# Odd chunks normalised before the second marker, and their loads moved in an mLSTM + FFN kernel

## The chip, the cores and the metric

The kernel runs on one core of a Trainium2 chip. Its time is device time in microseconds (us) for one launch. Engines are called as in the profile: PE is TensorE (PEld its weight loads), DVE is VectorE, ACT is ScalarE, POOL is GpSimd, SP is SyncE, which here only issues DMAs. Each engine works its own list of instructions strictly in order; an instruction that waits for a semaphore holds all that stand behind it on that engine.

## The reference

Two blocks are computed one after the other. The first is an mLSTM cell over 4 batches, 8 heads, 768 tokens and a head dimension of 40; the second is a feed-forward block with a squared ReLU, 3072 tokens by 320, with 2048 hidden units.

```python
# per batch and head, for every token t:
m_new = maximum(f_gate + m, i_gate)
f_stab = exp(f_gate + m - m_new);  i_stab = exp(i_gate - m_new)
C = f_stab * C + i_stab * outer(v, k)
n = f_stab * n + i_stab * k
y = sigmoid(o_gate) * (C @ q) / maximum(abs(n . q), 1)
# then, with x = y as (3072, 320):
h = maximum(x @ w_in, 0)
out = (h * h) @ w_out
```

Inputs and outputs are float32.

## The kernel before

The 3072 tokens are cut into 24 chunks of 128 tokens (six chunks per batch, all 8 heads of a chunk together). Within a chunk the recurrence is written as attention: scores k·q, weighted by exponentials of gate sums, plus the contribution of the state C that the chunk before left. The feed-forward block works on 12 groups of two chunks.

The main loop (L1440) goes through `parts`, four quarters (`at` 0 to 3) to a phase, one phase to a chunk s = 6, 7, 8, and so on. In even phases PE computes FFN2 of a group (seven products with sums of operands, `ffn2_fast`, L1066), in odd phases FFN1 of a later group (`ffn1_open` and `ffn1_close`, L1145 and L1178, twice each, also with sums of operands). The attention of the same chunk is woven in. The order on every engine is the order in which this loop writes the instructions down; no scheduler changes it. From chunk 10 on, even chunks are `joined` (L1437): the first half of their attention is done at the end of the odd phase before.

In the odd phase of chunk s (9 to 21) with `joined(s + 1)`, group g of FFN1:

- quarter 0: `ffn1_open(g, 0)`.
- quarter 1: attention of chunk s (`attend_begin`, first marker; `attend_end`), then on SP `store_num`, `load_A`, `load_num`: the numerators N of chunk s go to DRAM and come back turned. `ffn1_close(g, 0)`.
- quarter 2: weights of chunk s + 1, `ffn1_open(g, 1)`, the turn of the squares of k and q (`turn_kq`, L406), then S2 (`sums(g - 1, ..., (2,))`, L1056): S2 = S1 - A11, an operand of the second product of the next FFN2. POOL issues the loads of k and v of the even chunk s + 3.
- quarter 3: on SP `load_squares(s + 3)` (L399); `ffn1_close(g, 1)` with `attend_begin(s + 1)` in its middle. At the end of `attend_begin` stands a marker (L792): DVE reads the last number that PE has written and writes a spare word of k, which the next matmuls of the second half read; so this half starts behind the marker. Behind it DVE makes the four closing sums (L1192 to L1195). Then comes `normalise_turned(s)` (L890 to L903, nine DVE instructions: x = N, gated and divided), `store_rows(s)` (L931) and `load_o(s + 5)` (L414).

In the even phase of chunk s + 1 that follows:

- quarter 0: `attend_end(s + 1)`, then `mask` and `decay_C` of chunk s + 2 on POOL (L479, L768), the loads of k and v of the odd chunk s + 4 on POOL (L363 to L375, seven issues), and on SP `store_num(s + 1)`, `load_A(s + 3)`, `load_rows(s)` (L936, four issues: x of the odd chunk comes back from DRAM in squares), `load_num(s + 1)` (L878).
- quarter 2: `turn_squares(s)` on DVE (L943) finishes the turning of x; `normalise_turned(s + 1)`.
- quarter 3: `sums_of_x` on POOL (L1132, L1135) makes, from x of two chunks, the operands `xs` in `lent_t`, which the second block of matmuls of the next FFN1 reads (L1140).

Of the kernel before, what the change touches and what calls it, by code (L numbers as in the profile page):

```python
# [29 lines left out]
def kernel(  # L30
# [30 lines left out]
    NB = S // P  # L61
# [7 lines left out]
    NPAIR = NF // 2  # L69
# [853 lines left out]
    def xT_half(s):  # L923
        g, j = divmod(s, GT)
        if j == 0:
            st["xT", g] = xts.tile([P, GT, 3, P], F32, name="xT")
        return st["xT", g][:, j]

    def store_rows(s):
        t = st[s]["xT"] = xT_half(s).rearrange("p c t -> p (c t)")  # L930
        nc.sync.dma_start(x_d[s].rearrange("c t d -> t c d"), st[s]["x"][:].rearrange("p (c d) -> p c d", c=3))  # L931

    def load_rows(s):
        t = st[s]["xT"]
        for r in range(P // SQ):
            nc.sync.dma_start(  # L936
                t[r * SQ : (r + 1) * SQ].rearrange("p (b a) -> p b a", a=SQ),
                x_d[s, :, :, r * SQ : (r + 1) * SQ].rearrange("c (n p) a -> p (c n) a", p=SQ),
            )

    def turn_squares(s):
        t = st[s]["xT"]
        nc.vector.transpose(t, t)  # L943
        del st[s]
# [268 lines left out]
    def do(f, s):  # L1213
        if 0 <= s < NT:
            f(s)
# [97 lines left out]
    for u in range(8):  # L1313
        s = 2 + u // 2
# [122 lines left out]
    def joined(s):  # L1437
        return EARLY <= s < NT and s % 2 == 0

    for n, (which, g, i) in enumerate(parts):  # L1440
        s, at = NB + n // 4, n % 4
        if n == len(ROUNDED):
            brought.close()
            late = ctx.enter_context(tc.tile_pool(name="late", bufs=1, side="right"))
        even = s % 2 == 0
        fast = which == 1
        if n == 2:
            half_tanh(6)
            half_tanh(7)
        if at == 3 and not even and s + 3 > EARLY:  # L1450
            do(load_squares, s + 3)
        if at == 0 and even and s < EARLY:
            do(scores, s)
            if n > 0:
                do(turn_kq, s + 1)
            do(weighted, s)
        if n == 0:
            turn_kq(7)
            pair_up(8)
            load_rows(4)  # L1460
            rounding.words()
            rounding.join()
        if at == (0 if joined(s) else 1):
            if not joined(s):
                do(attend_begin, s)
            if n == 5:
                sums_of_weights(3)
            if even:
                do(lambda s: scores(s, ("h" if s < EARLY else False, "h")), s + 1)
            if fast:  # L1470
                ffn1_rows(g, 0, True)
                if joined(s + 1):
                    scores(s + 1, (False, "h"))
            do(attend_end, s)
            do(decays, s + 1)
            if not even and s > EARLY + 1:
                do(half_tanh, s)
            do(mask, s + 1)
            if not even and not fast:
                do(turn_kq, s + 1)  # L1480
            do(decay_C, s + 1)
            if not fast and not even:
                do(turn_squares, s - 1)
            if even and s > NB:
                do(load, s + 3)
            do(store_num, s)
            if s > NB + 1:
                do(load_A, s + 2)
            if joined(s):
                load_rows(s - 1)  # L1490
            if n == 1:
                normalise_turned(5)
                store_rows(5)
                turn_squares(4)
            if n == 5:
                load_rows(6)
            do(load_num, s)
            if n == 1:
                load_rows(5)
                weigh(7, masked=True)  # L1500
                sums_of_win(2)
            if s + 2 <= EARLY:
                do(load_squares, s + 2)
            if even and s <= NB + 1:
                do(load_A, s + 2)
        if n == 3:
            load_o(8)
            load_o(9)
            sums_of_weights(0)
        if n == 8:  # L1510
            sums(1, slice(0, NPAIR), (3,))
        if n == 9:
            sums(1, slice(0, NPAIR), (4,))
            sums_of_weights(2)
            turn_squares(6)
        if which == 2 and i == 3 and g == NG - 2:
            sums(g + 1, slice(0, NPAIR), (2,))
        if which == 2 and g > 1 and i < 2:
            sums(g, slice(0, NPAIR), (3 + i,))
        if at == 3 and even and NB < s and s // 2 - 1 < NG:  # L1520
            sums_of_x(s // 2 - 1)
        if at == 2 and not fast:
            if even and n > 2 and not joined(s):
                do(turn_squares, s - 1)
            do(scale_q, s + 1)
        if at == (1 if joined(s) else 3) and joined(s + 2):
            turn_kq(s + 2)
        if at == 3:
            if s % 4 == 3 and s < EARLY:
                for r in range(s + 1, min(s + 5, NT) if n > 7 else 10):  # L1530
                    half_tanh(r)
        if n == 10:
            half_tanh(10)
            half_tanh(11)
        if fast:
            if i % 2:
                if n == 7:
                    sums(1, slice(0, NPAIR), (2,))
                early = (lambda: attend_begin(s + 1)) if at == 3 and joined(s + 1) else None
                ffn1_close(g, i // 2, i == 1, early)  # L1540
                if early:
                    normalise_turned(s)
                    store_rows(s)
                    do(load_o, s + 5)
                if at == 1:
                    if s + 1 < EARLY:
                        do(turn_kq, s + 1)
                    if n > 5:
                        do(turn_squares, s - 1)
            else:  # L1550
                if at == 2 and joined(s + 1):
                    weigh(s + 1, masked=True)
                    weighted(s + 1)
                ffn1_open(g, i // 2)
                if at == 2 and joined(s + 1):
                    do(scale_q, s + 1)
                    do(turn_kq, s + 2)
                if i == (2 if joined(s + 1) else 0) and g > 2:
                    sums(g - 1, slice(0, NPAIR), (2,))
            if at == 2 and not joined(s + 1):  # L1560
                do(scale_q, s + 1)
            if n == 6:
                sums(1, slice(0, NPAIR), (1,))
        elif g == 0:
            ffn2(i)
        else:
            ffn2_fast(g, i)
        if at == 2:
            if n > 2 and not joined(s + 1):
                do(lambda s: weigh(s, masked=True), s + 1)  # L1570
            if even and s > EARLY:
                do(half_tanh, s)
            if even and s + 3 > EARLY:
                do(lambda s: load_squares(s, nc.scalar), s + 3)
            ffn1_square()
            if even and joined(s):
                do(turn_squares, s - 1)
            if even:
                do(weighted, s + 1)
            if not joined(s + 1):  # L1580
                do(normalise_turned, s)
                do(store_rows, s)
            if n == 2:
                pair_up(9)
                turn_squares(5)
                sums_of_x(2)
                load(8)
            if not even and s <= NB + 1:
                do(load_A, s + 2)
            if n > 2 and not joined(s + 1):  # L1590
                do(load_o, s + 5)
                do(load_rows, s)
            if s == NB + 1:
                pair_up(s + 3)
        if n in (5, 6):
            load(4 + n)
            load_o(5 + n)
        if at == 2 and joined(s + 1):
            do(load, s + 3)
        if n in (4, 7):  # L1600
            pair_up(11 + n // 7)
        if at == 3 and (even and s >= EARLY or s == EARLY - 1):
            for r in (5, 6) if even else (4, 5):
                do(pair_up, s + r)
        if n == 4:
            sums_of_weights(1)
        if n == 3:
            turn_halves()
        if n in (7, 16):
            spread_slots(2 + n // 16)  # L1610
        if at == 0:
            ffn1_square()
        if n < len(ROUNDED):
            while rounding.done < ROUNDED[n]:
                rounding.step()
# [30 lines left out]
```

## Time and profile before

| | |
|---|---|
| median of 3 runs | 489.94 us (489.55 to 490.25) |
| the profiled execution, its own time | 486.3 us |
| its span in the profile | 484.6 us |
| PE busy, of the span | 472.9 us (98%) |
| PE weight loads | 441.7 us (91%) |
| DVE busy | 340.2 us (70%) |
| ACT, POOL busy | 243.4 us (50%), 222.3 us (46%) |
| granted PE clock | 1.0 |

The profile is of one execution. Times in it count from the start of the span. A row of a timeline has start and length in us, engine, line of the kernel, operation, output<-input with their sizes, how many instructions are merged, and in brackets how long the engine was idle before it and what ended that. A row of waits has who waited for whom, then total us, how often, and the longest. SPq, POOLq and ACTq are the DMA issues of an engine. Chunks and phases can be told apart by time: the odd phases of chunks 9 to 21 end at about 166, 202, 240, 277, 312, 350 and 386 us.

### The profile page before, as it was taken

Reading aid. Unit: us, or ns where it says so; the run is one execution under the profiler, and the core shown is the slowest. Engines: PE = TensorE matmul, PEld = TensorE weight load, DVE = VectorE, ACT = ScalarE, POOL = GpSimd, SP = SyncE. Lnnn points to the kernel's source line nnn. Section 1 sums busy time; section 2 is a strip of 40 time slices with the busy share of each in tenths; the row PEclk is TensorE's granted clock in tenths of the full one; section 3 lists DMA queues with packets and bytes.
Section 4 is the critical chain, followed back from the end, with each engine's and each line's share of the span. In section 5 each row is a group of like instructions: output and inputs, shape, how many; then the busy total and the mean of one; then the engine's idle time right before and its main releaser. Section 6 shows DMA issues by size and latency. Waiting matters only on the chain.

```text
span 484.6 us, 15673 instructions
## 1 busy us (share of the span) xinstructions
PE 472.9 (98%) x6387; PEld 441.7 (91%) x6389; DVE 340.2 (70%) x725; ACT 243.4 (50%) x534; POOL 222.3 (46%) x337
## 2 busy tenths in 40 slices
PE   8999999999998999998999999999999999999997
PEld 5876788779998999998999999999999999999997
DVE  7969768898885966855965965865965957635441
ACT  4598798635743543544553552553553551513300
POOL 5464544677881866556556546554553111020000
DMA  8999998789995697596897696896694223200000
GB/s 177 218 248 252 273 212 219 223 141 230 204 181 142 137 190 184 95 168 134 157 173 171 119 171 146 145 174 138 123 160 97 70 76 84 55 23 7 1 28 27
DMA packets 192839, 69.93 MB, mean 144 GB/s; under 512 B 158144, under 2 KB 181504, under 8 KB 192768
## 3 DMA queue, kind: packets, MB, share of 16 engines
q1 hardware_dynamic: 157424, 56.39, 54.4%
q0 software_dynamic: 6080, 10.16, 9.4%
q10 hardware_dynamic: 29264, 2.39, 4.8%
q8 instruction: 50, 0.82, 0.7%
q14 instruction: 21, 0.17, 0.1%
HBM read 55.69 MB, written 18.92 MB: 154 GB/s over the span
## 4 chain that ended last, share of the span: by engine, by line
PE 79%; DMA 9%; DVE 5%; ACT 3%; issue 1%; POOL 1%; SPq 1%; DVEq 0%; POOLq 0%
PE h_ps L1061 27%; PE h_ps L1140 23%; PE h_ps L1173 7%; PE h_ps L977 4%; PE h_ps L1015 4%; DMA kqT<-kq_rows 3%; PE numT L823 3%; PE numT L801 2%; DMA kq<-num_rows 2%; DMA og<-in_o_gate_dram 2%; PE tp L587 1%; PE numT L835 1%; DMA A_bc<-a_slots 1%; PE h_ps L988 1%; PE tp L595 1%
## 5 line engine op out<-in xcount | busy, mean ns | idle before, releaser
L1061 PE MATMUL h_ps<-T,S 128*128 128x160 f32 x352 | 51.4, 299 | 0.0
L1061 PE MATMUL h_ps<-w_out,g 128*128 128x160 f32 x336 | 48.9, 301 | 0.7 <-issue 0.7
L1061 PEld LDWEIGHTS h_ps<-T,S 128*128 128x128 f32 x352 | 49.0, 190 | 0.0
L1077 DVE TENSOR_TENSOR y_sb<-y_sb,h_ps 128x160 f32<-128x160 f32 x44 | 14.0, 319 | 48.5 <-PE h_ps L1061 48.5
L1061 PEld LDWEIGHTS h_ps<-w_out,g 128*128 128x128 f32 x336 | 46.2, 190 | 1.9 <-issue 1.5
L1154 ACT COPY r_sb<-h_ps 128x512 f32<-128x512 f32 x20 | 11.7, 584 | 66.0 <-DMA kqT<-kq_rows 31.4
L1140 PE MATMUL h_ps<-xT,w_in 128*128 128x128 f32 x320 | 43.3, 278 | 0.0
L1140 PE MATMUL h_ps<-lent_t,w_in 128*128 128x128 f32 x320 | 42.3, 275 | 0.0
L1173 PE MATMUL h_ps<-xT,w_in 64*64 64x128 f32 x960 | 39.5, 272 | 1.7 <-DVE r_sb L1156 1.7
L1140 PE MATMUL h_ps<-lent_t 128*128 128x128 f32 x320 | 39.2, 276 | 1.6 <-POOL lent_t L1135 1.6
L1140 PEld LDWEIGHTS h_ps<-xT,w_in 128*128 128x128 f32 x320 | 39.2, 192 | 1.6 <-issue 1.2
L1140 PEld LDWEIGHTS h_ps<-lent_t 128*128 128x128 f32 x320 | 37.3, 192 | 2.0 <-POOL lent_t L1135 2.0
L375 POOL DMA_DIRECT2D va<-in_v_dram x64 | 39.1, 621 | 0.0
L1140 PEld LDWEIGHTS h_ps<-lent_t,w_in 128*128 128x128 f32 x320 | 38.9, 192 | 0.0
L1132 POOL TENSOR_TENSOR lent_t<-xT 128x128 f32<-128x128 f32 (+1 forms) x18 | 10.2, 590 | 60.0 <-DVE xT L943 36.0
L1173 PEld LDWEIGHTS h_ps<-xT,w_in 64*64 64x64 f32 x960 | 35.1, 133 | 2.5 <-DVE r_sb L1156 2.0
L479 POOL TENSOR_SCALAR_AFFINE_SELECT A_bc<-A_bc 64x512 f32<-64x512 f32 x32 | 23.6, 737 | 28.8 <-ACT kq L497 25.8
L510 ACT ACTIVATE A_bc<-A_bc,b_R 128x64 f32<-128x64 f32 (+1 forms) x128 | 35.6, 363 | 0.1
L1191 ACT ACTIVATE g<-h_ps 128x512 f32<-128x512 f32 x12 | 7.2, 597 | 54.0 <-PE h_ps L1140 36.7
L768 POOL TENSOR_TENSOR Cd<-C,kq 128x164 f32<-128x164 f32 x15 | 13.9, 930 | 43.4 <-DVE C L865 37.5
L858 DVE STREAM_TRANSPOSE tn<-numT 128x256 f32<-128x256 f32 x36 | 14.0, 426 | 23.5 <-PE numT L801 15.5
L977 PE MATMUL h_ps<-xT,w_in 128*128 128x256 f32 x128 | 29.9, 386 | 0.4 <-POOL w_in L236 0.4
(231 smaller groups left out, 1201.8 us busy)
## 6 DMA issues: line engine op xcount, KB each, us to landing
A_bc<-a_slots SPq DMA_DIRECT2D x32, 256.0 KB, 4.3
kq<-num_rows SPq DMA_DIRECT2D x80, 64.0 KB, 3.5
num_rows<-tn SPq DMA_DIRECT2D x18, 256.0 KB, 2.6
raw<-in_moe_w_out_dram SPq DMA_DIRECT2D x7, 640.0 KB, 5.4
og<-in_o_gate_dram SPq DMA_DIRECT2D x24, 160.0 KB, 5.1
x_rows<-x_sb SPq DMA_DIRECT2D x20, 192.0 KB, 2.4
xT<-x_rows SPq DMA_DIRECT2D x80, 48.0 KB, 3.5
out_dram<-y_sb SPq DMA_DIRECT2D x23, 160.0 KB, 2.5
```

Of the source, the lines that this page charges most:

```text
L375: eng.dma_start(dst[HALVES[n], PR * (1 - late_keys) : PR * (2 - late_keys)], src[HALVES[late_keys], PR * m : PR * (m + 1)],)
L479: nc.gpsimd.affine_select(part, part, compare_op=ALU.is_ge, fill=-1e30, base=0, pattern=[[0, PR], [0, 2], [1, DP]], channel_multiplier=-1,)
L510: nc.scalar.activation(A[0][:, x, to], A[0][:, x, to], AF.Exp, bias=b_R[:, b, c, own, x : x + 1],)
L768: nc.gpsimd.tensor_tensor(Cd, C_b[(s - 1) % 2][:, : PR * D1].rearrange("p (j d) -> p j d", d=D1), st[s]["eA"][:, :, P - 1 : P].to_broadcas ...
L823: nc.tensor.matmul(d["numT"][m][DP * e : DP * e + wide, i, t0:], lhsT=va_w[s % NKQ][keys, at * D1 : at * D1 + wide], rhs=rhs, start=(s % N ...
L858: nc.vector.transpose(to[:, 2 * m : 2 * m + 2], d["numT"][m].rearrange("p c t -> p (c t)"))
L977: nc.tensor.matmul(hs[i][:, n, :], lhsT=w_in[:, a, fb * P : (fb + 1) * P], rhs=xT[:, :, a, :], start=(n == 0 and a == 0), stop=False,)
L1015: nc.tensor.matmul(st["o_ps"][j], lhsT=st["g2", 0][:, fb, j * P : (j + 1) * P], rhs=w_out[:, fb, :], start=(fb == 0), stop=(fb == NF - 1),)
L1061: nc.tensor.matmul(to, lhsT=lhsT[:, p], rhs=rhs[:, p, :], start=(start and p == 0), stop=(p == NPAIR - 1), skip_group_check=True,)
L1077: add = lambda to, a, b: nc.vector.tensor_tensor(to, a, b, op=ALU.add)
L1140: nc.tensor.matmul(to[:, n, :], lhsT=lhsT[:, 4 * q + n, :], rhs=rhs, start=(start and n == 0), stop=True, skip_group_check=True,)
L1173: nc.tensor.matmul(to[cols, n, :], lhsT=w_in2[rows, 4 * q + n, cols], rhs=rhs, start=(start and n == 0), stop=True, skip_group_check=True,)
```

## The change

For the odd chunks s = 9 to 21, four things move; nothing is added and nothing taken away.

1. `normalise_turned(s)`, `store_rows(s)` and `load_o(s + 5)` go from behind the closing sums of quarter 3 to quarter 2, behind `turn_kq`, where S2 stood. They are now ahead of the second marker.
2. S2 goes from there to behind the closing sums.
3. `load_rows(s)` goes from the even phase (between `load_A` and `load_num`) to the odd phase, behind `load_squares(s + 3)`.
4. The loads of k and v of chunk s + 4 go from the start of the even phase to the end of the odd phase (for chunks 13 to 23; chunk 11's stay where they were).

```diff
         if at == 3 and not even and s + 3 > EARLY:
             do(load_squares, s + 3)
+            if joined(s + 1):
+                load_rows(s)
...
-            if even and s > NB:
-                do(load, s + 3)
+            if s == NB + 2:
+                load(s + 3)
             do(store_num, s)
             if s > NB + 1:
                 do(load_A, s + 2)
-            if joined(s):
-                load_rows(s - 1)
...
                 ffn1_close(g, i // 2, i == 1, early)
                 if early:
-                    normalise_turned(s)
-                    store_rows(s)
-                    do(load_o, s + 5)
+                    sums(g - 1, slice(0, NPAIR), (2,))
...
                 if at == 2 and joined(s + 1):
                     do(scale_q, s + 1)
                     do(turn_kq, s + 2)
-                if i == (2 if joined(s + 1) else 0) and g > 2:
+                    normalise_turned(s)
+                    store_rows(s)
+                    do(load_o, s + 5)
+                if i == 0 and g > 2 and not joined(s + 1):
                     sums(g - 1, slice(0, NPAIR), (2,))
...
         if at == 3 and (even and s >= EARLY or s == EARLY - 1):
             for r in (5, 6) if even else (4, 5):
                 do(pair_up, s + r)
+        if at == 3 and joined(s + 1):
+            do(load, s + 4)
```

## The prediction

> **What bounds the kernel now.** I read the page first, then the waits of TensorE and its weight loads from 90 us on, then the timeline around the longest wait that the change touches, then an undisturbed place of the same kind.
>
> ```profile
> span 484.6 us, 15673 instructions
> ...
> PE 472.9 (98%) x6387; PEld 441.7 (91%) x6389; DVE 340.2 (70%) x725; ACT 243.4 (50%) x534; POOL 222.3 (46%) x337
> ```
>
> TensorE is busy for 472.9 of 484.6 us, so no reordering can gain more than 11.7 us, and most of that lies in the start. The waits from 90 us on say what is left to gain:
>
> ```profile
> PE h_ps L1173 <- DVE r_sb L1156: 1.7, 1, 1.7
> ...
> PEld h_ps L1140 <- POOL lent_t L1135: 2.0, 2, 1.5
> ...
> PEld h_ps L1061 <- issue: 1.5, 5, 0.8
> ...
> PEld numT L835 <- issue: 0.3, 1, 0.3
> ```
>
> The first lies at 148 us, ahead of the first moved instruction, and stays. The second is what the change can reach: weight loads of the first FFN1 quarter wait 2.0 us, in two places (0.47 us at 182.4, 1.52 us at 218.4), for POOL's sums of x. The last two (0.80 us at 312.5, 0.32 us at 239.5) end with nothing that the profile shows. The timeline at the longer of the two places:
>
> ```profile
> 207.04 0.53 SPq L873 DMA_DIRECT2D num_rows<-tn  x1
> 208.87 2.09 SPq L936 DMA_DIRECT2D xT<-x_rows  x4
> 211.00 5.67 SPq L878 DMA_DIRECT2D kq<-num_rows  x4
> ...
> 215.59 0.32 DVE L1077 TENSOR_TENSOR y_sb<-y_sb,h_ps 128x160 f32<-128x160 f32 x1 [0.72 <-PE h_ps L1061]
> ...
> 217.63 0.58 DVE L943 STREAM_TRANSPOSE xT<-xT 128x384 f32<-128x384 f32 x1 [1.72 <-DMA xT<-x_rows]
> ...
> 218.34 1.14 POOL L1132 TENSOR_TENSOR lent_t<-xT 128x128 f32<-128x128 f32 x2 [5.58 <-DMA kqT<-kq_rows]
> ...
> 219.44 0.45 POOL L1135 TENSOR_TENSOR lent_t<-lent_t,xT 128x128 f32<-128x128 f32 x1
> ...
> 219.94 1.86 PEld L1140 LDWEIGHTS h_ps<-lent_t 128*128 128x128 f32 x16 [1.52 <-POOL lent_t L1135]
> ```
>
> The reader is to see a chain of four: the odd chunk's x is reloaded by issues from 208.87 on, the last data are there at 217.6, VectorE turns it (0.58), POOL sums it (1.14 + 0.45), and TensorE has waited 1.52 us. POOL's own wait is put down to a kqT transfer by the profile; the turn, done 0.13 us before, is what it needed. The same order where TensorE does not wait, in the phase of chunk 15:
>
> ```profile
> 271.71 2.54 SPq L399 DMA_DIRECT2D kqT<-kq_rows  x4
> 272.76 1.18 DVE L1056 TENSOR_TENSOR S<-S,g_c 128x1024 f32<-128x1024 f32 x1
> 274.02 0.16 DVE L792 TENSOR_SCALAR kq<-numT 1x1 f32<-1x1 f32 x1
> 274.94 0.69 DVE L1192 TENSOR_TENSOR r_sb<-r_sb,h_ps 128x512 f32<-128x512 f32 x1 [0.76 <-PE h_ps L1173]
> ...
> 276.74 0.68 DVE L1195 TENSOR_TENSOR g<-r_sb,h_ps 128x512 f32<-128x512 f32 x1
> 277.34 0.32 DVE L890 TENSOR_SCALAR dm<-kq 128x8 f32<-128x8 f32 x1
> ...
> 279.13 2.23 PEld L1061 LDWEIGHTS h_ps<-T,S 128*128 128x128 f32 x16
> ```
>
> Here S2 (L1056) stands in the slot that the normalisation is to take, and 279.13 is when TensorE first needs S2.
>
> **The change, part by part.** It acts in the seven odd phases of chunks 9, 11, ... 21. The orders of TensorE's and ScalarE's instructions stay as they are; VectorE, SP and POOL are reordered, and nothing is added or taken away.
>
> *Odd x earlier: the gain.* The nine normalising instructions (277.34 to 279.42, 2.08 us) go to S2's old slot, so x is stored about 4.5 us earlier and reloaded before the even phase begins. For chunk 11: normalised by about 200.7, stored by 201.1, behind it on SP one load of o (0.5), four load_squares issues (2.54) and four reloads (2.09): the last reload is issued by about 207 and lands by about 212, if it takes the 3.5 us median; even the 6.9 us that it took at 209 gives 214. VectorE turns x right behind L1077 (215.91), at 215.83 instead of 217.63. POOL's two steps then end at 218.09; the weight load that needs them would come at 218.43, when the eight before it are through. Both waits go: 0.47 + 1.52 = 2.0 us. Late next is the POOL sum, with 0.34 us to spare, the same as at 292.8 in the phase of chunk 15, which does not wait.
>
> *Normalising ahead of the marker: a cover of about zero.* From slot to L1192 there are 2.18 us (272.76 to 274.94; also 235.98 to 238.17, 345.45 to 347.64, 381.82 to 384.00), and 2.6 us for chunks 11 and 17. Into it must go 2.08 us and the marker, which is followed after 0.1 us. So the closing sums start about 0.05 us late, if the numerators N are there. The second half of the attention, which waits for the marker on TensorE, starts at 276.21, 1.1 us after the marker's new end (275.0). N must have landed by the slot. The landings of the last of its four issues (L878) against the slots: chunk 9, 160.1 and 162.0; 11, 198.5 and 197.87; 13, 237.6 and 235.98; 15, 271.7 and 272.76; 17, 309.1 and 308.07; 19, 343.7 and 345.45; 21, 380.5 and 381.82. Three of seven are late, by 0.6, 1.6 and 1.0 us. For 13 and 17 SP was held: the reload of even x (225.83, 3.28 us; 298.78) waited for chunk 12's or 16's store, which was late behind an even N (0.82 us of wait at 219.93) or slow to land (4.1 us from 294.70). Both come from the crowded even phase, which the change thins out (below), so I take 13 as on time and 17 as half as late, and 11 as it was, 0.7 us from slot to start.
>
> *S2 behind the closing sums.* S2 takes 1.18 us and is pipelined to about 1.15. Closing sums end at 277.42, plus 0.05, plus 1.15: 278.6 against 279.13, 0.5 us to spare. For chunk 11 the marker slips to 200.7, L1192 from 200.43 to 200.8, S2 ends at 204.4, and TensorE wants it at 204.39: cost 0 to 0.2, taken 0.1. Chunk 17 stands 0.6 us of lateness without cost (0.4 before L1192, 0.3 behind S2, 0.1 to start), and pays 0.4 at its full 1.0: taken 0.1. Chunk 13 at its full 1.6 would pay 0.75 (S2 done at 243.5, wanted at 242.76). In exchange the transposes of the even numerators lose 2.08 us ahead of them and gain 1.15: they come 0.9 us earlier.
>
> *SP.* Seven times, four reload issues (1.86 to 2.4 us) leave the even phase, where they stood ahead of load_num, which waited behind them: even N is loaded about 2.5 us earlier. store_rows and load_o move ahead of load_squares of the next even chunk, which now waits for the normalising and goes from 271.71 to about 275.9. With 2.54 us of issues and 3.7 us of landing (to about 281 or 282) it still precedes its turn on VectorE at 283.08, behind which lie 1.67 us of idle time before L1077 at 285.98. Cost nothing; without that cover, the excess.
>
> *POOL.* Six times, the seven issues of odd k and v (0.79 + 1.23 + 2.44 = 4.46 us) move ahead of the mask. In chunk 15's phase POOL is free at 272.85, so the mask slips from 276.18 to 277.3; ScalarE wants it at 284.0. The tightest is chunk 9's, where eight kq_rows issues end at 166.30: mask done at 172.2, wanted at 173.24. No cost. The buffers were last read by the attention of the same chunk, over 8 us earlier.
>
> *DMA.* The moved transfers land where the engines were idle (at 276 to 280 us they moved 5 GB/s) and leave a crowded stretch. But this is the stretch in which TensorE runs small matmuls, and its instructions are fetched through the same engines: the windows 236 to 240 and 310 to 314 each show one 16 KB fetch, DMA engines that are full until 238 and 311.4, and one of the two waits ended by "issue". load_squares, the thickest of that traffic, now goes behind these two fetches, odd k and v ahead of them. Bounds: all 1.12 us (0.80 + 0.32) gone, or three such fetches (chunks 13, 17, 21) stretched to about 1.3 us of wait each, 3.9 - 1.1 = 2.8 us more. I take 0.3 us gone, since load_squares fills more of the time there than the POOL queue does (78.1% against 20.6%).
>
> [...]
>
> **Sum.** -2.0 + 0.1 + 0.1 - 0.3 = -2.1 us, on the profiled execution's 486.3 us (484.6 of span and 1.7 around it): 484.2. The median shown, 489.94, is 3.6 us above that execution, so 487.8.
>
> **Rivals.**
> 1. *The numerators are not there (slower).* At their new place the normalising instructions stand ahead of the marker and the closing sums. Against it: four of seven N have landed by then, and the three late ones, left as late as they are, cost 0.1 + 0.75 + 0.4 = 1.3 us and leave a gain of 1.0. For it: the stores and loads moved into this quarter could delay N. It decides when N lands more than 0.5 us behind the slot as a rule. At chunk 13's lateness in all seven phases: 7 x 0.75 = 5.2, less 2.0 and 0.3: +2.9, 492.8 us.
> 2. *Instruction fetches suffer (slower).* The upper bound above: +2.8 - 2.0 + 0.1 = +0.9, 490.8 us.
> 3. *The wait moves on (no change).* The turn or POOL's sums miss the 0.34 us, or the even phase's squares come late and hold L1077, so that what is won at 182 and 218 us is lost elsewhere: 489.9 us. For it: all covers here are below 1 us. Against it: chunk 15's phase runs with the same covers.
>
> **How the numbers follow.** Main case 0.60, its own range 486.4 to 488.9 (3.1 gained with both "issue" waits and few late N at one end, 1.0 with N as late as before at the other; 0.4 for the spread of the runs shown at the fast end). Rival 3: 0.19. Rival 2: 0.11. Rival 1: 0.10. A measurement tells 0.2%, 1.0 us, from no change. Faster: 0.60 and a little of rival 3, 0.62; same: 0.19; slower: rivals 1 and 2 less what falls inside 1 us, 0.19. The range goes from 486.4 to 491.3: above it lie rival 1 and a little of rival 2, below it some 0.07.
>
> **What would show it.** Right: no wait of L1140 for lent_t; xT turned at once behind L1077 in every even phase; the normalising not waiting for N by more than 0.5 us. Wrong: weight loads of T,S waiting for S2, L835 waiting for the marker, DVE waiting at L406 for kqT, or "issue" waits over 1.1 us in all.

## The result, and the profile after

| | median | ratio to before (95%) |
|---|---|---|
| before, 20 runs | 490.12 us (487.13 to 492.88) | |
| after, 20 runs | 487.47 us (484.65 to 491.49) | 0.9951 (0.9927 to 0.9974) |

The changed kernel is faster by 0.49% (0.26 to 0.73%), some 2.4 us. From the page of after, the span and the busy times:

```profile
span 488.2 us, 15700 instructions
...
PE 476.6 (98%) x6389; PEld 444.6 (91%) x6389; DVE 344.1 (70%) x725; ACT 244.0 (50%) x534; POOL 224.9 (46%) x337
```

By this page alone the kernel would have become slower: 488.2 us of span against 484.6. The profiled execution took 489.91 us, more than the median of its kernel, and what it lost lies ahead of the first moved instruction: a half clock for 6.8 us around 33 us, a wait of 1.0 us at 104.9 and one of 2.0 us at 133, none of which the profile of before has. So the two spans are not to be compared. What can be compared is a stretch in which TensorE has the same work in both kernels, from the first FFN2 product (L1061) in the phase of chunk 10 to the end: 484.6 - 166.2 = 318.4 us before, 488.2 - 170.5 = 317.7 us after. A second trace of each (below) gives 319.9 and 316.7. The mean difference is 1.93 us.

The waits of the weight loads from 160 us on, in after (who waited for whom, total us, how often, longest):

```profile
PEld h_ps L1061 <- PE h_ps L1061: 0.9, 1, 0.9
...
PEld numT L835 <- DVE kq L792: 0.6, 1, 0.6
PEld h_ps L1061 <- issue: 0.5, 3, 0.2
PEld numT L823 <- issue: 0.5, 2, 0.3
```

The line of 2.0 us for lent_t is gone, and so are the two "issue" waits of 0.80 and 0.32 us; 0.35 us of that kind are left, at L823. Two lines are new, 0.9 for S2 and 0.6 for the marker. The timeline of after at the place where before waited longest for lent_t (start, length, engine, line, operation; in brackets the idle time before it and its releaser):

```profile
220.94 0.32 DVE L1077 TENSOR_TENSOR y_sb<-y_sb,h_ps 128x160 f32<-128x160 f32 x1 [0.72 <-PE h_ps L1061]
221.17 0.57 DVE L943 STREAM_TRANSPOSE xT<-xT 128x384 f32<-128x384 f32 x1
...
222.98 0.45 POOL L1135 TENSOR_TENSOR lent_t<-lent_t,xT 128x128 f32<-128x128 f32 x1
...
223.69 1.87 PEld L1140 LDWEIGHTS h_ps<-lent_t 128*128 128x128 f32 x16
```

VectorE turns the odd x right behind L1077, where before it had waited 1.72 us for the reload; POOL's sum is there at 223.43 and the weight load at 223.69 waits for nothing.

The two new lines are both of chunk 11. The timeline of after there:

```profile
203.88 0.17 DVE L890 TENSOR_SCALAR dm<-kq 128x8 f32<-128x8 f32 x1 [2.24 <-DMA kq<-num_rows]
...
205.84 0.16 DVE L792 TENSOR_SCALAR kq<-numT 1x1 f32<-1x1 f32 x1
206.03 0.69 DVE L1192 TENSOR_TENSOR r_sb<-r_sb,h_ps 128x512 f32<-128x512 f32 x1
206.05 0.32 PEld L835 LDWEIGHTS numT<-vw,kq 64*64 64x64 f32 x16 [0.62 <-DVE kq L792]
...
208.43 1.22 DVE L1056 TENSOR_TENSOR S<-S,g 128x1024 f32<-128x1024 f32 x1
...
209.76 2.20 PEld L1061 LDWEIGHTS h_ps<-T,S 128*128 128x128 f32 x16 [0.91 <-PE h_ps L1061]
```

The first normalising instruction waits 2.24 us for N; the marker behind it makes the second half of the attention 0.62 us late, and S2, two steps further on, the second FFN2 product 0.91 us (the profile names TensorE's own product there; S2 ended at 209.65, 0.1 us before). The waits of the matmuls, in place of those of the weight loads, name S2 itself:

```profile
PE h_ps L1061 <- DVE S L1056: 0.7, 1, 0.7
```

Together the weight loads lose 1.53 us.

### The profile page after: what moved, and what is told of

Same layout as the page of the kernel before. It is cut to its first block, busy times and chain, and to the rows that moved or that the text cites. A ratio compares the mean times of both kernels' runs of the same rounds, so it can differ in the third digit from the quotient of the medians.

```text
span 488.2 us, 15700 instructions
## 1 busy us (share of the span) xinstructions
PE 476.6 (98%) x6389; PEld 444.6 (91%) x6389; DVE 344.1 (70%) x725; ACT 244.0 (50%) x534; POOL 224.9 (46%) x337
## 4 chain that ended last, share of the span: by engine, by line
PE 77%; DMA 10%; SPq 6%; DVE 3%; ACT 1%; issue 1%; POOL 0%; DVEq 0%; ACTq 0%; POOLq 0%
PE h_ps L1061 32%; PE h_ps L1140 22%; PE h_ps L1173 7%; PE h_ps L977 5%; DMA kqT<-kq_rows 3%; PE numT L823 3%; DMA kq<-in_q_dram 2%; PE numT L801 2%; SPq L399 2%; PE tp L587 1%; PE h_ps L988 1%; DMA xT<-x_rows 1%; PE numT L835 1%; DMA raw<-in_moe_w_in_dram 1%; SPq L206 1%
## 5 line engine op out<-in xcount | busy, mean ns | idle before, releaser
L1061 PE MATMUL h_ps<-T,S 128*128 128x160 f32 x352 | 51.6, 300 | 0.7 <-DVE S L1056 0.7
L1061 PEld LDWEIGHTS h_ps<-T,S 128*128 128x128 f32 x352 | 48.9, 190 | 1.1 <-PE h_ps L1061 0.9
L1061 PE MATMUL h_ps<-w_out,g 128*128 128x160 f32 x336 | 48.8, 302 | 0.0
L1061 PEld LDWEIGHTS h_ps<-w_out,g 128*128 128x128 f32 x336 | 46.2, 190 | 1.1 <-issue 0.5
L1077 DVE TENSOR_TENSOR y_sb<-y_sb,h_ps 128x160 f32<-128x160 f32 x44 | 14.0, 318 | 45.2 <-PE h_ps L1061 45.1
L1140 PE MATMUL h_ps<-xT,w_in 128*128 128x128 f32 x320 | 43.2, 278 | 0.0
L1140 PE MATMUL h_ps<-lent_t,w_in 128*128 128x128 f32 x320 | 42.3, 275 | 0.0
L1140 PEld LDWEIGHTS h_ps<-xT,w_in 128*128 128x128 f32 x320 | 39.2, 192 | 1.6 <-issue 1.2
L1140 PE MATMUL h_ps<-lent_t 128*128 128x128 f32 x320 | 39.1, 275 | 0.0
L1140 PEld LDWEIGHTS h_ps<-lent_t,w_in 128*128 128x128 f32 x320 | 39.0, 192 | 0.0
L1140 PEld LDWEIGHTS h_ps<-lent_t 128*128 128x128 f32 x320 | 37.3, 192 | 0.2 <-issue 0.2
L479 POOL TENSOR_SCALAR_AFFINE_SELECT A_bc<-A_bc 64x512 f32<-64x512 f32 x32 | 25.7, 802 | 17.0 <-ACT kq L497 15.8
L977 PE MATMUL h_ps<-xT,w_in 128*128 128x256 f32 x128 | 31.6, 402 | 0.0
L531 POOL TENSOR_TENSOR vw<-va,A_bc 128x328 f32<-128x328 f32 x13 | 11.5, 886 | 39.6 <-ACT A_bc L510 39.6
```

Of the source, the lines that this page charges most:

```text
L479: nc.gpsimd.affine_select(part, part, compare_op=ALU.is_ge, fill=-1e30, base=0, pattern=[[0, PR], [0, 2], [1, DP]], channel_multiplier=-1,)
L531: nc.gpsimd.tensor_tensor(d["vw"][:].rearrange("p (own x) d -> p own x d", own=2), d["va"][:].rearrange("p (own x) d -> p own x d", own=2) ...
L977: nc.tensor.matmul(hs[i][:, n, :], lhsT=w_in[:, a, fb * P : (fb + 1) * P], rhs=xT[:, :, a, :], start=(n == 0 and a == 0), stop=False,)
L1061: nc.tensor.matmul(to, lhsT=lhsT[:, p], rhs=rhs[:, p, :], start=(start and p == 0), stop=(p == NPAIR - 1), skip_group_check=True,)
L1077: add = lambda to, a, b: nc.vector.tensor_tensor(to, a, b, op=ALU.add)
L1140: nc.tensor.matmul(to[:, n, :], lhsT=lhsT[:, 4 * q + n, :], rhs=rhs, start=(start and n == 0), stop=True, skip_group_check=True,)
```

## Experiments

In each group the kernels ran on one chip and share the runs of before on it. The theory was the prediction's: the gain is the wait for POOL's sums of x, and it goes because the odd x is reloaded earlier. The rivals: the loads of k and v, taken out of the even phase, do it alone; and the loss at chunk 11 comes from those loads, or from N standing ahead of the marker.

**The two kernels once more.** After as it is:

> The change as it is, executed again on the chip on which its parts are tried, so that they can be compared with it. The gain was 0.49% (0.26 to 0.73). My theory: 2.0 us of weight-load waits for POOL's sums of x are gone, and chunk 11 gives 0.1 to 1.6 us back, because its numerators N land up to 2.2 us behind the slot at which they are normalised; so -0.5 to -2.5 us, and a trace with no wait of L1140 for lent_t and a wait at L835 for the marker, or at L1061 for S2, in chunk 11's phase. Rival (chance): the wait of chunk 11 was of that one execution, and is not seen again.

486.17 us (12 runs), ratio 0.9978 (0.9950 to 1.0006): on this chip the times alone do not tell the change from before. The lent_t line is absent again, and no "issue" wait above the usual 0.2 us is left. Chunk 11 lost again. Waits of the weight loads, then VectorE's timeline there:

```profile
PEld h_ps L1061 <- PE h_ps L1061: 1.2, 1, 1.2
```

```profile
199.43 0.29 DVE L890 TENSOR_SCALAR dm<-kq 128x8 f32<-128x8 f32 x1 [1.17 <-DMA kq<-num_rows]
...
204.19 1.69 DVE L1056 TENSOR_TENSOR S<-S,g 128x1024 f32<-128x1024 f32 x1
```

N was 1.17 us late, and S2 took 1.69 us in place of 1.22; why it was longer was not looked into. Before, one more trace:

> The kernel before, looked at once more, to see which of its waits belong to it and which to one execution. My theory: the weight loads of L1140 wait again for POOL's sums of x at chunk 10's and 12's phase ends, 1.5 to 2.5 us in all, and there is no wait of L835 for the marker or of L1061 for S2 in chunk 11's phase. Rival (the 2.0 us were chance): no such wait above 0.5 us.

488.31 us. Its waits:

```profile
PEld h_ps L1140 <- POOL lent_t L1135: 2.7, 3, 1.4
PEld h_ps L1061 <- issue: 1.8, 5, 1.1
```

So the wait that the change removes was 2.0 us in one trace of before and 2.7 in the other, and the two "issue" waits at 240 and 313 us together 1.12 and 1.34 us. Two further kernels below keep the old order and show this wait with 2.0 and 0.7 us. What follows: the gain and the losses repeat, and their sizes move from execution to execution, that of the gain by up to 2 us.

**Without the early loads of k and v** (part 4 undone):

```diff
-            if s == NB + 2:
-                load(s + 3)
+            if even and s > NB:
+                do(load, s + 3)
...
-        if at == 3 and joined(s + 1):
-            do(load, s + 4)
```

> The change without its fourth part: odd k and v are loaded at the start of the even phase, as before; everything else as changed. My theory (the gain comes from normalising and reloading the odd x early): the waits for the sums of x stay away, -2.0 us, and chunk 11's N are less late than in the change (0.6 us as before instead of 2.2), so 0.1 instead of 1.6 us is lost there: -2 to -3 us, faster than before by 0.4 to 0.6%. Rival (the gain comes from the thinner even phase, that is from the loads): at most -0.5 us, no change that can be told.

487.61 us, ratio 1.0001 (0.9972 to 1.0030). No wait for lent_t, so parts 1 to 3 remove it without part 4. The loss at chunk 11 stayed and grew:

```profile
PEld numT L835 <- DVE kq L792: 1.0, 1, 1.0
PEld h_ps L1061 <- PE h_ps L1061: 0.9, 1, 0.9
```

N(11) came 2.30 us late with the loads of k and v in their old place: these loads are not what delays it.

**The early loads alone** (before with part 4, and nothing else):

> The kernel before with the fourth part alone: odd k and v are loaded at the end of the odd phase, normalising, S2 and reload stay where they were. My theory: the reload of x is still issued behind store_num and load_A at about 209 us of the trace of before, and lands 1 to 2 us earlier in a thinner phase, so the 1.5 us wait shrinks to 0 to 1 and the 0.5 us one goes: -0.5 to -1.5 us. Rival (the loads are what counts): -2 us or more, all of the gain.

487.66 us, ratio 0.9994 (0.9966 to 1.0021). No wait for lent_t either. SP's timeline at the reload of chunk 11's x, with VectorE's turn of it:

```profile
212.11 2.07 SPq L936 DMA_DIRECT2D xT<-x_rows  x4
```

```profile
219.23 0.57 DVE L943 STREAM_TRANSPOSE xT<-xT 128x384 f32<-128x384 f32 x1
```

The reload stands in its old place in the even phase, 7.1 us ahead of the turn (in before, 7.0 us ahead of the time at which VectorE was free for it), but the data came in time; before they had needed 8.7 us from 208.87 to 217.6. What the prediction took for the gain, the earlier reload, isn't needed to remove the wait: taking seven issues' worth of k and v out of the same stretch is enough. The stretch from chunk 10's FFN2 on is 317.5 us, as in after. In turn, the "issue" waits stayed, the first of them at another place (23.9 us after the first FFN2 product of chunk 12's phase, before 37.7):

```profile
PEld numT L835 <- issue: 1.2, 1, 1.2
PEld h_ps L1061 <- issue: 1.2, 4, 0.7
```

Neither half can be told from before by its time in these runs. In both traces a cost that has nothing to do with the edit, 3.4 and 6.8 us of half clock at 150 us, stands in the span; more on it below.

**The late reload** (after without part 3):

```diff
-            if joined(s + 1):
-                load_rows(s)
...
+            if joined(s):
+                load_rows(s - 1)
```

> The change without its third part: odd x is normalised and stored early and odd k and v are loaded early, but x is reloaded in the even phase between load_A and load_num, as before. The trace of the loads alone showed no wait for the sums of x, so I expect none here: x is stored 4 us earlier still. Chunk 11's N are normalised at the same early place, so 1 to 2 us of TensorE's wait for the marker and S2 stay. Even N come later than in the change by the four reload issues (2 us), and at chunk 12 the normalising waits for them. Rival (the reload's place is what removes the wait): L1140 waits 1 us or more for lent_t.

488.82 us, one run. No wait for lent_t. Nothing lost at chunk 11, against what was expected: N(11) was 0.35 us late there, which cost TensorE nothing. S2 was late by 0.91 us at chunk 17 (the first line), whose N came 1.65 us late, and there was one "issue" wait:

```profile
PEld h_ps L1061 <- PE h_ps L1061: 0.9, 1, 0.9
...
PEld numT L835 <- issue: 0.7, 1, 0.7
```

The stretch is 317.2 us, within those of after (316.7 and 317.7). So the third part is worth nothing that a trace can tell once the two others are there.

**Chunk 13's loads back in the even phase of chunk 10**, to see whether these delay N(11) (`if s in (NB + 2, EARLY): load(s + 3)`, and the new loads from `s > EARLY` on):

> The change, but chunk 13's k and v are loaded at the start of chunk 10's phase as before; from chunk 11's phase on the loads move as in the change. In the trace of the change the four issues of load_squares in chunk 9's phase took 5.79 us beside these loads (2.69 before), the reload behind them came at 175.2, N of chunk 10 landed 1.4 us late and N of chunk 11 2.2 us late, and TensorE lost 0.70 + 0.86 us. My theory: with these seven issues out of the way load_squares takes about 3 us again, N of chunk 11 is late by less than 1 us, and the loss there falls from 1.6 to at most 0.4 us: 1 to 1.5 us faster than the change, 0.6 to 0.8% faster than before. Rival (chunk 11's N are late because of the traffic of its own phase, or it was chance): no difference from the change.

486.68 us, ratio 0.9971 (0.9943 to 0.9998). N(11) was still 1.73 us late:

```profile
PEld h_ps L1061 <- PE h_ps L1061: 0.9, 1, 0.9
...
PEld numT L835 <- DVE kq L792: 0.3, 1, 0.3
```

0.91 + 0.34 = 1.25 us lost. I had put the loss on these loads; that theory fell, here and in the first of the halves. What is left is the order itself: N stands ahead of the marker, and N(11) isn't there.

**Chunk 11 in the old order**, all else as after:

```diff
-            if joined(s + 1):
+            if joined(s + 1) and s != EARLY + 1:
                 load_rows(s)
...
+            if s == EARLY + 2:
+                load_rows(s - 1)
...
-                if early:
+                if early and s != EARLY + 1:
                     sums(g - 1, slice(0, NPAIR), (2,))
+                elif early:
+                    normalise_turned(s)
+                    store_rows(s)
+                    do(load_o, s + 5)
...
+                    if s == EARLY + 1:
+                        sums(g - 1, slice(0, NPAIR), (2,))
+                    else:
+                        normalise_turned(s)
...
```

> The change, but chunk 11 alone keeps the old order of normalising, S2 and reload (its successors' loads still move). In four traces with the early normalising, TensorE waited 1.2 to 1.9 us at chunk 11 for the marker and for S2, because DVE waited 1.2 to 2.3 us for N. My theory: this wait goes, and the wait for the sums of x at chunk 12, which this order had before (1.5 us), does not come back, since it was absent with the loads alone: 1.2 to 1.9 us faster than the change, so 0.5 to 0.9% faster than before. Rival: the wait for the sums of x returns, and the time is the change's.

485.58 us (9 runs), ratio 0.9954 (0.9930 to 0.9979). Waits from 160 us on:

```profile
PEld h_ps L1140 <- issue: 0.9, 5, 0.2
PEld numT L823 <- issue: 0.7, 2, 0.5
```

The first is the usual sum of five short ones that every trace here has. Both waits of chunk 11 are gone, the wait for lent_t didn't come back, and the stretch is 315.9 us, the shortest of all. So the loss comes from N standing ahead of the marker when it is late. In the next kernel, which keeps this order for chunk 11, N(11) landed later than in any other trace (34.1 us after the first FFN2 product of chunk 10's phase), and nobody waited for it.

**The wait at 148 us.** Before and all kernels so far wait there, and the prediction had set this wait aside. VectorE's timeline of before:

```profile
147.63 1.25 DVE L406 STREAM_TRANSPOSE kqT<-kqT 128x1024 f32<-128x1024 f32 x1 [2.53 <-DMA kqT<-kq_rows]
148.80 0.28 DVE L1077 TENSOR_TENSOR y_sb<-y_sb,h_ps 128x160 f32<-128x160 f32 x1
149.01 0.68 DVE L1156 TENSOR_TENSOR r_sb<-h_ps,r_sb 128x512 f32<-128x512 f32 x1
```

The turn of chunk 10's squares (L406) waits for a transfer, and behind it stand three additions, among them the one that TensorE waits for (L1156). It is the same pattern as at chunk 11: one waiting instruction holds all behind it. On top of the last kernel, this turn was moved behind the additions:

```diff
-        if at == (1 if joined(s) else 3) and joined(s + 2):
+        if at == (1 if joined(s) else 3) and joined(s + 2) and s != NB + 2:
...
                 # behind ffn1_open
+                if s == NB + 3 and at == 0:
+                    turn_kq(EARLY)
```

> The kernel of the last run with one more edit: the turn of chunk 10's squares of k and q stands on DVE behind the two additions of the next FFN1 quarter instead of ahead of them. In every trace so far, of before too, DVE waits 1.6 to 3.6 us there for the squares, with the additions queued behind the wait, and TensorE waits 1.8 to 3.1 us for an addition (at about 148 us); in three of six traces the granted clock then falls to half for 3.4 to 6.8 us. My theory: that wait goes and with it the fall of the clock: 2 to 5 us faster than the kernel without the edit, 1.0 to 1.8% faster than before. Rival: the wait moves to the scores of chunk 10, which read the turned squares, and 0 to 0.5 us are won.

482.69 us, ratio 0.9903 (0.9874 to 0.9931). The wait at 148 is gone. The next one in line shows at once:

```profile
PEld h_ps L1061 <- PE h_ps L1061: 1.4, 2, 0.7
PEld numT L835 <- DVE kq L792: 1.0, 1, 1.0
```

Chunk 9's phase now begins sooner, its N does not, and it loses 0.99 + 0.69 us as chunk 11 had done; the other 0.68 is at 348.5. The same edit on before, without any of the change:

> The kernel before with the later turn of chunk 10 alone. It prices this edit without the change. My theory: TensorE's wait for the addition at about 148 us (1.4 to 3.1 us in ten traces) goes, and with it the half clock behind it where that came: -2 to -3.5 us. Rival: -0.5 us at most, the wait moves to the scores of chunk 10 or to N of chunk 9.

485.50 us (10 runs), ratio 0.9930 (0.9905 to 0.9956), with the waits of before left as they were:

```profile
PEld h_ps L1140 <- POOL lent_t L1135: 2.0, 2, 1.7
PEld h_ps L1061 <- issue: 1.6, 5, 1.0
```

So this one turn is worth about as much as the whole change, 0.7% against 0.5%; the two intervals overlap.

**The best of both.** Chunks 9 and 11 in the old order, the later turn, the rest as after (`s > EARLY + 1` in place of `s != EARLY + 1` above):

> The later turn of chunk 10, and the change with the old order of normalising, S2 and reload for chunks 9 and 11; the new order from chunk 13 on, odd loads moved for all. With the later turn the phase of chunk 9 starts 2 us sooner, and there DVE waited for N of chunk 9 as it had for chunk 11 (TensorE: 0.99 + 0.69 us). My theory: these 1.7 us go as well, 1.1 to 1.4% faster than before. Rival (the wait for the sums of x at chunk 10 returns, 0.5 to 1.4 us): the time of the kernel with chunk 11 alone in the old order, 1.0%.

483.14 us, ratio 0.9885 (0.9847 to 0.9923); of what the edits touch only one "issue" wait is left (0.63 us at 310.2). And before with the early loads and the later turn alone:

> The later turn of chunk 10 and the loads of odd k and v at the end of the odd phase, nothing else of the change: normalising, S2 and reload in the old order in all seven phases. It tells what normalising early is worth from chunk 13 on, against the kernel with the old order for 9 and 11 alone. My theory: the loads alone keep the sums of x in time, so all that is lost against that kernel are the waits that end with issue at about 230 to 240 and 315 us, 1.9 us in the trace of the loads alone against 0.5 there: 1 to 1.5 us slower than it. Rival (early normalising from 13 on is worth nothing): equal times.

483.44 us, ratio 0.9883 (0.9851 to 0.9915):

```profile
PEld h_ps L1061 <- issue: 1.4, 3, 1.1
PEld numT L835 <- issue: 1.4, 1, 1.4
```

It has the "issue" waits that the other lacks, 1.35 and 1.06 us, and its stretch is longer, 317.8 against 316.1 us; the times can't be told apart, so no gain of normalising the odd chunks early is shown. Beside the later turn alone (0.9930, on the same chip) the loads of k and v give another 0.5%: each of the six runs (482.62 to 484.43 us) is below each of the ten (484.51 to 487.53). There the part of the change that removes the wait for lent_t shows in the time by itself.

**What the "issue" waits are.** Before, with 40 more tiny matmuls at the very start (`idle(12, 40)`), so that every later instruction of TensorE stands elsewhere in its list:

> The kernel before with 40 more tiny matmuls among the idle ones at the start, so that each later instruction of TensorE stands 80 places further on (each matmul has a weight load). If the waits ended by issue at about 240 us (L835) and 314 us (L1061) are waits for instructions fetched in blocks, the same blocks now end 80 instructions earlier in the work: the waits move forward into the scores or the rows ahead of them (L587, L1173), or vanish where the block ends in a stretch of long matmuls. If they belong to the work itself (a bank, an operand, a queue), they stay at L835 and L1061 with 0.3 and 0.8 to 1.1 us.

490.50 us, one run. At 240 and 313 us nothing is left of these waits; they stand now at 206.5 (1.31), 267.8 (1.20) and 281.6 (0.44):

```profile
PEld numT L823 <- issue: 3.0, 3, 1.3
```

and once at 114.4 us (1.35, L1140). The work around them is the same, only the place in the list has changed. I read them as waits for instructions. The page of before has a DMA queue for these (packets, MB, share of 16 engines' span):

```profile
q8 instruction: 50, 0.82, 0.7%
```

In both places of that trace TensorE has gone on 1.3 us after the end of one of its 16 KB packets (packet to 238.64, wait to 239.91; to 312.24 and 313.56). The 50 packets stand against 12941 instructions of TensorE and its weight loads, one for every 259; counted over these instructions, 20 of the 21 "issue" waits above 0.25 us that lie behind 90 us, over all fourteen traces, stand 192 to 194 places behind a multiple of 256 (in before, instructions 6336 and 8640). Of the 43 packets behind 90 us in before, these two have such a wait (0.32 and 0.80 us) and 41 have none; over the traces single ones cost 0.3 to 1.35 us.

## Why the prediction was right, and where it was not

The size was right, 487.8 predicted, 487.47 measured, and so was the main term. That the sum came out so close is luck: chunk 11 cost 1.3 us more than taken, and the wait, the fetches and chunk 17 together gave 1.2 us more.

| term, us | predicted | traces: before | after |
|---|---|---|---|
| wait for POOL's sums of x | -2.0 | 2.0; 2.7 | 0; 0 |
| chunk 11 | +0.1 | 0; 0 | 1.53; 1.23 |
| chunk 17 | +0.1 | 0; 0 | 0; 0 |
| "issue" | -0.3 | 1.12; 1.34 | 0.35; 0 |
| sum | -2.1 | 3.1; 4.0 | 1.9; 1.2 |

By the means this is 1.55 - 3.6 = -2.0 us, and the stretches gave -1.93.

- *Odd x earlier: the gain.* Shown, as to the wait: chunk 11's x was in at 216.06, 45.6 us after the phase's first FFN2 product (the forecast, 212 against 166.2, says 45.8, though its own terms, 207 and 3.5 us, give 210.5; the agreement is luck, as the last issue came at 43.3 us in place of 40.8 and landed in 2.3 us in place of 5), the turn follows L1077 in every even phase, and POOL's margin was 0.26 us where I had 0.34. Not shown, as to the cause: the loads alone (part 4), parts 1 to 3 without them, and parts 1, 2 and 4 without the earlier reload each remove the same wait. The parts overlap, and the prediction's words, that the gain is that of "odd x earlier", gave it all to one of them. In the times only the loads showed a gain by themselves, with the later turn in place.
- *Normalising ahead of the marker: a cover of about zero.* The step that failed is "11 as it was, 0.7 us from slot to start", and "cost 0 to 0.2, taken 0.1" with it. The gain and the loss were costed one by one: once the wait at 182 us is gone, chunk 11's slot comes 0.5 us sooner (31.2 in place of 31.6 us after the first FFN2 product of the phase), and N does not. N itself landed at 33.3 and 32.2 us, against 32.3 and 33.9 in the two traces of before. So VectorE waited 2.24 and 1.17 us for it, where I had 0.6. Why its landing moves so much stays open; that the loads of k and v are not the whole reason was shown. The early reload goes with a late landing: in the four traces with odd loads moved throughout and chunk 9's x reloaded in the even phase (loads alone, late reload, the last two kernels) N(11) landed at 31.4 to 31.6 us, in the six with the early reload at 31.7 to 34.1, and in the four with neither at 31.5 to 33.9. Among those with the early reload are two without chunk 13's early loads, so this is a pattern over a few traces and no test, and no group of runs prices it. If it holds, the part that the prediction took for the gain feeds the loss. Chunk 13 was on time as taken (landed 239.46, slot 239.98), and so was 17, of which half was expected late (311.25, 311.71).
- *S2 behind the closing sums* cost nothing where N was on time. Rival 1 had the mechanism right; its condition held at one chunk of seven, at chunk 9 when the phase was made to start sooner, and at 17 with the late reload.
- *SP: "even N is loaded about 2.5 us earlier"* was wrong. SP's timeline of after at the end of chunk 9's phase and the start of chunk 10's:

```profile
168.30 0.38 SPq L931 DMA_DIRECT2D x_rows<-x_sb  x1
168.72 0.49 SPq L414 DMA_DIRECT2D og<-in_o_gate_dram  x1
169.32 5.79 SPq L399 DMA_DIRECT2D kqT<-kq_rows  x4
175.21 3.53 SPq L936 DMA_DIRECT2D xT<-x_rows  x4
...
181.08 1.73 SPq L878 DMA_DIRECT2D kq<-num_rows  x4
```

  The four issues of load_squares, 2.69 us at this place in the trace of before, take 5.79 us here (in chunk 11's phase 4.09 in place of 2.84), and what stands behind them on SP waits. The issue of even N came 0.6 to 2.7 us later against the first FFN2 product of its phase (chunk 10: 8.0 to 10.6; 12: 8.8 to 10.1; 14: 7.4 to 9.3; 16: 7.8 to 8.5). Chunk 10's N landed later as well (15.8 to 16.4), and VectorE waited 1.42 us for it, before 0.05. From chunk 12 on the time from issue to landing was shorter, so that N landed earlier all the same (17.6 to 15.8; 15.1 to 14.9; 15.1 to 12.7). Nobody on TensorE waited. The mistake was to take the length of an issue from one place (chunk 15, 2.54 us); the trace of before has 4.63 us in chunk 13's phase.
- *POOL, mask* and the turns of squares: no wait of TensorE for either in both traces, as said. But from 160 us on VectorE waited at L406 three times in each trace of after (1.65, 0.67 and 0.31 us in the first), and never in those of before: this sign of being wrong was seen, as were the waits for the marker and for S2, and only the cover kept it free.
- *DMA and the fetches.* The bounds held (all of 1.12 gone; 0.8 and 1.3 were), the value taken was low. That load_squares, sent behind the fetches, is the reason is in keeping with the loads alone leaving these waits at 1.25 and 0.69 us, and with 0 to 1.0 us wherever the normalising was moved; with waits that also depend on the place in TensorE's list (40 more matmuls at the start moved them from 240 and 313 us to 206.5, 267.8 and 281.6) it isn't proved. One reading in the prediction was off: in the window 236 to 240 the DMA engines were busy until about 239.2 us, with a dip at 238.

## What to carry to other kernels

What stood behind a waiting instruction on its engine was late with it here: VectorE's 2.24 us for N(11) held the marker and S2 and cost TensorE 1.53 us, its 2.53 us for the squares of chunk 10 held the additions behind them and cost 1.98. Before moving an instruction that waits for a transfer, ask not only whether its data were there in the old trace, but when the slot comes once the gain of the change has been taken: chunk 11's slot came 0.5 us sooner, and its N landed at 33.3 and 32.2 us after the phase's first FFN2 product, against 32.3 and 33.9 in before. When several edits come together, run each alone before the gain is given to one of them; here moving seven DMA issues was enough (no wait for lent_t, in before 2.0 and 2.7 us). And read spans of two profiles only from a common instruction on, as the part ahead of the change can differ by more than the change is worth (170.5 us after, 166.2 before, against a gain of some 2.4).

## What the runs showed of the hardware

The wait at 148 us can cost more than its length. Windows of 4 us, in the kernel with the loads alone, where it lasted 3.1 us, and in before, where it lasted 2.0 (columns: window, us, then busy time and instructions of PE, PEld, DVE, ACT, POOL, the granted clock, the DMA share, GB/s):

```profile
148.00:152.00 4.00, 1.16 (x21) 1.07 (x24) 2.90 (x5) 0.00 (x0) 0.00 (x0) 0.73 0.61 119
152.00:156.00 4.00, 4.00 (x99) 4.00 (x92) 0.00 (x0) 0.00 (x0) 0.00 (x0) 0.50 0.27 68
156.00:160.00 4.00, 4.00 (x62) 3.82 (x58) 2.06 (x6) 1.87 (x6) 0.46 (x1) 0.91 0.26 98
```

```profile
148.00:152.00 4.00, 2.26 (x87) 2.26 (x90) 2.53 (x5) 0.00 (x0) 0.00 (x0) 1.00 0.64 127
152.00:156.00 4.00, 4.00 (x86) 3.83 (x79) 2.00 (x6) 1.81 (x6) 0.46 (x1) 1.00 0.27 101
```

In the first the clock falls to 0.50 for 6.83 us. Over the traces, with the gap taken from one matmul's start to the next one's: after gaps of 1.4 to 1.8 us (four traces) the clock stayed full; after one of 2.01 us it was half for 3.41 us, after 2.36 and 2.86 us for 3.41 us each, after 3.11 us for 6.83 us; but after 2.01 (before) and 2.11 us (after) it stayed full. So a gap of about 2 us may or may not cost another 1.7 us (half of 3.41), with the same instructions: from the FFN2 product at about 132 us to the first of chunk 10's phase, before took 34.17 us and the second trace of after 35.85, with gaps of 2.01 us both. Behind this wait the half clock came for 3.41 us or twice that; what decides whether it comes, these traces do not show: in after it also came at 33.3 us, for 6.83 us, where the longest gap from 25 us on was 0.96 us.

That time was 33.6 to 38.0 us over the traces that have the wait, a spread of 4.4 us; the 17 runs of before in the last group go from 486.6 to 492.2. With the turn moved the runs on the same chip spread less, 482.5 to 485.5 and 482.6 to 484.4 (six each) and 484.5 to 487.5 (ten). That the clock makes most of that spread fits this, but no run shows it by itself.
